# Small-pass evictions shared by ScalarE and VectorE, two additions and one lower sum moved to GpSimd

## The chip, the cores and the metric

The kernel runs on one core of a Trainium2 chip. A core has a matmul engine (PE in the profile, with PEld for the loading of its weights), VectorE (DVE), ScalarE (ACT), GpSimd (POOL), which also issues most of the DMAs here, and SP, which issues the rest. Each engine runs its own list of instructions in the order in which the program wrote them, and semaphores tie the lists together. PE writes only to PSUM, eight banks of 512 float32 values in each of 128 partitions; DVE and ACT read them from there. The metric is the device time in microseconds (us). Before the change it is 955.75 us, the median of three runs (955.62 to 957.78).

## The reference

The input x is 8 batches of 4224 rows of 192 values, float32. First comes a causal convolution along the rows with 7 taps, one set of taps for each of 8 heads of 24 columns; then layer normalisation without a bias, a 192 to 768 to 192 multilayer perceptron with ReLU, and a residual addition.

```python
w = softmax(weight)                              # (8 heads, 7 taps)
y[s, h] = sum(w[h, k] * x[s - 6 + k, h] for k in range(7))
xn = (y - mean(y)) / sqrt(var(y) + 1e-06) * g_ln
out = y + maximum(xn @ w_ch1, 0.0) @ w_ch2
```

## The kernel before, in words

The rows are split over the 128 partitions and worked on in 18 groups; a normal group g has 16 rows in each partition. The kernel works in float32. It folds the mean and g_ln into the first weight matrix, and applies 1/sqrt(var) only at the end, since ReLU lets a positive factor pass.

Groups 3 to 17 are "mixed" (`MIXED`): both matrix products are done by a Strassen-like scheme, with 7 products of quarter matrices in place of 8, and sums of quarters before and after. A mixed group has two stages on PE.

**Up** (`up_mixed`, L611, matmuls on L533) multiplies by the first weights in two passes. The small pass (`one`) makes one block of 128 hidden columns for each quarter: seven products of 24 matmul instructions. The large pass (`two`) makes the other two blocks: seven products of 48. The products go in turn to two sets of four PSUM banks, X and Y, so that PE writes one set while the other is evicted. Some products add to what the other set keeps. After each product ScalarE copies the four banks to the hidden tile `a` (`evict`, L640, its copies on L651). Where two results must be added, the copy goes to a scratch place and POOL issues an accumulating DMA (`close` and `add_by_dma`, L653 and L608), or DVE adds from PSUM (L657).

**Down** (`down_fast`, L833, matmuls on L850) multiplies the hidden tile by the second weights, again with seven products. Before the second, `lower_sum` (L821) has put relu(c21) - c11 in place of c21, in three blocks of 1024 elements a partition. During the fourth product DVE makes three half sums (L817), which the fifth product needs, and then six more. ScalarE copies the results to `cs` (L856), and the fifth and sixth products to `parts`, in places of the hidden tile that are free by then.

The engines do other work at the same time, and its place is written out by hand:

- DVE: taps 2 to 6 of the convolution of group g+1 (`conv`, L417, through `taps_of_next`) in the large pass of g; the transpose of g+1 (L428) in down, ahead of the half sums; at the end of down the sums of quarters s1 and s2 of the next group (`sums_of_y`, L600 and L601) and the batch statistics of its 16 rows (`moments`, L448); then, in the small pass of the next group, `finish_fast` (L908): for either half one addition of `parts` to `cs` (L912) and three transposes to the result tile `ot` (L914).
- ScalarE: the first two taps of group g+2, behind the evictions of down; the ReLUs; the scaling of the finished group by 1/sqrt(var).
- POOL: s3 and s4 (L605, L606), made to wait for DVE's s2 by a tiny memset (L604); the accumulating DMAs: y<-tb (second tap, L409), those of `close`, and those that add the result to the output (L940); in every second group the reciprocal square root for two groups (`root`, `pending`), a chain of some 20 small operations.

`finish_fast` reaches the next group through a generator: `ahead(g)` does both halves when the small pass has been written (L700: `next(ahead)`), so on DVE they come behind the statistics and before the taps of the large pass. The last group (`last`) already shares its small pass, two banks each, between ScalarE and DVE.

Of the kernel before, what the change touches and what calls it, by code (L numbers as in the profile page):

```python
# [11 lines left out]
ALU = mybir.AluOpType  # L12
# [4 lines left out]
def kernel(  # L17
# [29 lines left out]
    nc = tc.nc  # L47
    PSUM = bass.MemoryType.PSUM
    B, S, D = x.shape
    H, K = weight.shape  # L50
# [12 lines left out]
    NQ = P // C  # L63
# [19 lines left out]
    PAIR = NF // 2 - 1  # L83
    HJ = J // 2
    EARLY = 10
    CH = NC // 2
    FC = NF // 2
# [37 lines left out]
    def take_set():  # L125
        i = (turn[0] + 3) // 4 * 4 % 8
        turn[0] = i + 4
        return all_banks[:, i : i + 4]
# [99 lines left out]
    low = consts.tile([P, 1], F32, name="low")  # L228
# [364 lines left out]
    def sums_of_y(g, engine):  # L593

        room = upool.tile([P, 3 * HJ * CH * C], F32, tag="ys", name=f"ysums{g}")
        room = room.rearrange("p (v j c t) -> p v j c t", v=3, c=CH, t=width(g))
        s1, s2, s3 = [room[:, v] for v in range(3)]
        a11, a12, a21, a22 = quarters_of_y(g)
        ysums[g] = s1, s2, s3, a21
        nc.vector.tensor_tensor(s1, a21, a22, op=ALU.add)  # L600
        nc.vector.tensor_tensor(s2, s1, a11, op=ALU.subtract)  # L601
        if engine is not nc.vector:

            nc.vector.memset(s3[:, 0:1, 0:1, 0:1], 0.0)  # L604
        engine.tensor_tensor(s3, a21, a11, op=ALU.subtract)  # L605
        engine.tensor_tensor(a21, a12, s2, op=ALU.subtract)  # L606
# [4 lines left out]
    def up_mixed(g, ahead, pending):  # L611
# [11 lines left out]
        class Pass:  # L623
# [15 lines left out]

            def evict(self, banks, dst, relu=False, f=None):  # L640
                src = self.seen(banks, f)
                if last and self.n == 1:
                    near, far = [[v[:, :, q : q + 2] for v in (dst, src)] for q in (0, 2)]
                    if relu:
                        nc.scalar.activation(*near, AF.Relu)
                        nc.vector.tensor_scalar_max(*far, 0.0)
                    else:
                        nc.scalar.copy(*near)
                        nc.vector.tensor_copy(*far)
                    return  # L650
                nc.scalar.activation(dst, src, AF.Relu) if relu else nc.scalar.copy(dst, src)  # L651
# [23 lines left out]
        def taps_of_next(*args, **kw):  # L675
            if not last:
                conv(g + 1, *args, **kw)


        X, Y = take_set(), take_set()  # L680
        one, two = Pass(PAIR, FC, X, Y), Pass(0, PAIR, Y, X)
        p = one
        p.product(X, a11, p.b11, True, False)
        p.evict(X, p.c11)
        p.product(Y, a12, p.b21)
        p.close(p.c11, Y, two.c12[:, 0:1])
        next(pending, None)
        p.product(X, s2, p.t[0], False, False)
        p.evict(X, p.c21)
        p.product(Y, s3, p.t[1], True, False)  # L690
        p.evict(Y, p.c22)
        p.product(X, s1, p.b12, False, False)
        p.close(p.c22, X, two.c12[:, 1:2])
        next(pending, None)
        p.product(Y, a22, p.t[2], False)
        p.close(p.c21, Y, two.c22[:, 0:1])
        p.product(X, s4, p.b22, False)
        p.evict(X, p.c12, True)

        next(ahead)  # L700
        p = two
        rooms = parts(cpool, "cs"), parts(bpool, "tb")
        p.product(Y, a11, p.b11, True, False)
# [37 lines left out]
        if last:  # L741
            one.relu(one.c22)
        else:
            lower_sum(g, (PAIR,))
            taps_of_next(5, 6, heads=(H // 2, H - 1))
        p.close(p.c21, X)
        if last:
            lower_sum(g, (PAIR,))
# [5 lines left out]
        if last:  # L754
# [9 lines left out]
                nc.scalar.activation(kept[:, f, :, :, h], src, AF.Relu)  # L764

            keeping = [lambda f=f, h=h: keep(f, h) for f in range(NF) for h in range(2)]
        taps_of_next(5, 6, heads=(H - 1, H))
        taps_of_next(6, K)

        def scale_one(j):  # L770
# [47 lines left out]
                a[:, *dst, f], a[:, *left, f], a[:, *right, f], op=op  # L818
            )

    def lower_sum(g, fs=range(FC)):  # L821

        a = of_products(g)
        if g in MIXED:
            for f in fs:
                nc.vector.scalar_tensor_tensor(
                    out=a[:, 1, 0, f], in0=a[:, 1, 0, f], scalar=0.0, in1=a[:, 0, 0, f],
                    op0=ALU.max, op1=ALU.subtract,
                )
        else:  # L830
            half_sum(g, (1, 0), (1, 0), (0, 0), ALU.subtract, fs)

    def down_fast(g, work):  # L833
        n = fast[g]
        t = width(g)
        w = n * T
        a = of_products(g)
        flat = cpool.tile([P, NC, NFAST * C], F32, tag="cs", name=f"cs{g}")[:, :, 0 : n * C]
        order = "p c (h j t) -> p c h j t" if t == C else "p c (j h t) -> p c h j t"
        cs = flat.rearrange(order, h=2, t=t)  # L840
        free = a[:, 1, 0].rearrange("p f q j t -> p (f q) j t")
        parts = [free[:, 0:CH], free[:, CH : 2 * CH]]
        banks = [take_bank() for c in range(CH) for i in range(2)]

        def product(bank, left, right, to, first, behind=0):
            for c in range(CH):
                dst = banks[2 * c + bank]
                for f in (PAIR, *range(PAIR)):
                    for q in range(NQ):
                        nc.tensor.matmul(  # L850
                            dst[C * q : C * q + C, 0:w], right[:, f, C * c : C * c + C],
                            left[:, f, q], start=(first and f == PAIR), stop=(f == PAIR - 1),
                            skip_group_check=True,
                        )
                if to is not None:
                    nc.scalar.copy(  # L856
                        to[:, c], dst[:, 0:w].rearrange("p (j t) -> p j t", t=t)
                    )
                for one in work[:behind]:
                    one()  # L860
                del work[:behind]

        b = quarters_of_w2()
        c11, c21 = cs[:, 0:CH, 0], cs[:, 0:CH, 1]
        c12, c22 = cs[:, CH:NC, 0], cs[:, CH:NC, 1]
        if g == 2:
            work += [lambda h=h: first_tap(4, heads=(h, h + 1)) for h in range(7, H)]
            work += [lambda h=h: second_tap(4, heads=(h, h + 1)) for h in range(H)]
        elif g + 2 < NG:
            work += [  # L870
                lambda tap=tap, h=h: tap(g + 2, heads=(h, h + 1))
                for tap in (first_tap, second_tap) for h in range(H)
            ]
        behind = (1, 1, 1, 1) if g == 2 else (3, 2, 2, 3)
        if g + 1 == NG:
            behind = (0, 0, 1, 2)
        product(0, a[:, 0, 0], b[0], c11, True, behind[0])
        product(1, a[:, 1, 0], w2sums[:, 2], c22, True, behind[1])
        product(1, a[:, 1, 1], w2sums[:, 3], c21, False, behind[2])
        product(1, a[:, 0, 1], b[2], None, True, behind[3])  # L880
        if g + 1 < NG:
            transpose(g + 1)
            if g == 2:
                b11, b12 = quarters_of_w1()[0:2]
                nc.vector.tensor_tensor(b12, b12, b11, op=ALU.subtract)
        half_sum(g, (1, 1), (1, 1), (1, 0), ALU.add)
        half_sum(g, (0, 0), (1, 1), (0, 0), ALU.add)
        half_sum(g, (0, 1), (0, 1), (1, 1), ALU.subtract)
        for c in range(CH):
            nc.vector.tensor_tensor(  # L890
                c11[:, c], c11[:, c], banks[2 * c + 1][:, 0:w].rearrange("p (j t) -> p j t", t=t),
                op=ALU.add,
            )
        product(0, a[:, 1, 1], w2sums[:, 1], parts[0], False, 2)
        product(0, a[:, 0, 0], w2sums[:, 0], parts[1], False, 2)
        for one in work:
            one()
        product(0, a[:, 0, 1], b[3], c12, False)
        if g + 1 < NG:
            sums_of_y(g + 1, nc.gpsimd)  # L900
            if g == 2:
                load_x(5, gate=True)
            moments(g + 1)
        else:
            finish_fast(g, 0, flat, cs, parts)
        return flat, cs, parts

    def finish_fast(g, half, flat, cs, parts):  # L908
        n = fast[g]
        ot = ots[g] if half else out_tile(g)  # L910
        fresh = cs[:, CH * half : CH * half + CH, 1]
        nc.vector.tensor_tensor(fresh, fresh, parts[half], op=ALU.add)  # L912
        for c in range(CH * half, CH * half + CH):
            nc.vector.transpose(  # L914
                ot[:, 0:n, C * c : C * c + C], flat[:, c].rearrange("p (j t) -> p j t", t=C)
            )

    ots = {}

# [76 lines left out]
    def ahead(g):  # L996


        if results is not None:
            for half in range(2):  # L1000
                finish_fast(g - 1, half, *results)
        yield

    w11, w12, w21, w22 = quarters_of_w1()
    b11, b12, b21, b22 = quarters_of_w2()
# [100 lines left out]
```

## Time and profile before

| what | value |
|---|---|
| median of three runs | 955.75 us |
| the profiled execution | 956.96 us |
| its span, first to last instruction | 954.6 us |
| PE, DVE, ACT, POOL busy | 946.8, 894.2, 694.8, 341.8 us |
| up and down stage of a usual mixed group | 27.96 and 27.44 us |
| ACT, eviction of 128x1024 from PSUM (L651), each | 1.013 us |
| DVE, addition of parts (L912), each | 0.929 us |
| DVE, lower sum of one block (L826), each | 1.221 us |
| POOL, 128x768 sum (L605, L606), each | 1.83, 1.82 us |

A line of the trace in order of time gives the start from the beginning of the span, the duration, the engine, the line of the kernel, the operation, what it writes and reads with its shape, and how many such instructions are merged; in brackets stands how long the engine had been idle before, and what ended that wait. Durations of successive DVE instructions overlap by some 0.1 us, so the distance from start to start is the better price of one. A busy PE need not be at its peak, since matmuls are pipelined. A wait is read as: engine and line that waited, what it waited for, us in total, times, longest.

### The profile page before, as it was taken

The page shows a single profiled execution, that of the slowest core. Times are in us where ns is not written, and L with a number is a line of the kernel's source. Part 1 is how long each engine was busy: PE and PEld are TensorE (multiplying, and loading weights), DVE is VectorE, ACT ScalarE, POOL GpSimd, SP SyncE. Part 2 cuts the span into 40 slices and gives each one's busy share as a digit, 9 for nine tenths or more (in the row PEclk, how much of TensorE's full clock was granted, in tenths as well). Part 3 has the DMA queues.
Part 4 walks back from the last instruction along what each step waited for, and adds up shares of the span by engine and source line. Part 5 has one row for each costly group of instructions (what it writes and reads, how often), then busy time and mean ns, then how long its engine had stood idle before and what let it go on. Part 6 is the DMA issues. An engine that isn't in the chain of part 4 may idle for free.

```text
span 954.6 us, 37896 instructions
## 1 busy us (share of the span) xinstructions
PE 946.8 (99%) x16858; PEld 734.5 (77%) x16858; DVE 894.2 (94%) x1496; ACT 694.8 (73%) x1166; POOL 341.8 (36%) x474
## 2 busy tenths in 40 slices
PE   8999999999999999999999999999999999999998
PEld 7998896877869687786958778695867769586787
DVE  8999999999999999999999999999999999999867
ACT  7764678596877959687796968779695877967362
POOL 1158422613145141533227141452316232261330
PEclk9999999999999999999999999999999999999999
DMA  8359589689696988979697897969889697778261
GB/s 206 111 151 218 110 233 269 122 188 226 130 273 131 251 158 185 221 130 278 126 252 152 199 215 128 277 133 249 158 198 206 124 275 134 174 135 141 40 122 68
DMA packets 39832, 169.34 MB, mean 177 GB/s; under 512 B 4469, under 2 KB 8182, under 8 KB 33655
## 3 DMA queue, kind: packets, MB, share of 16 engines
q0 software_dynamic: 32864, 106.77, 60.2%
q1 hardware_dynamic: 6800, 60.16, 17.4%
q8 instruction: 132, 2.16, 0.9%
q14 instruction: 30, 0.25, 0.1%
q10 hardware_dynamic: 6, 0.00, 0.0%
HBM read 38.93 MB, written 50.33 MB: 94 GB/s over the span
## 4 chain that ended last, share of the span: by engine, by line
PE 96%; DMA 1%; POOL 1%; ACT 1%; issue 0%; DVE 0%; ACTq 0%; POOLq 0%
PE ps L533 46%; PE ps L850 44%; PE ps L787 4%; PE ps L367 1%; DMA room<-room 1%; DMA out_dram<-y 1%; PE ps L326 1%; ACT room L651 0%; POOL room L609 0%; POOL d L460 0%; ACT y L380 0%; POOL r L483 0%; POOL d L478 0%; POOL d L479 0%; PE ps L335 0%
## 5 line engine op out<-in xcount | busy, mean ns | idle before, releaser
L417 DVE SCALAR_TENSOR_TENSOR y<-xg,taps,y 128x384 f32<-128x384 f32 (+3 forms) x720 | 364.8, 583 | 2.6 <-DMA y<-room 1.4
L850 PE MATMUL ps<-room,w2sums 128*32 128x256 f32 (+2 forms) x4608 | 246.6, 371 | 0.0
L533 PE MATMUL ps<-yt,w 32*128 32x256 f32 (+2 forms) x4104 | 234.7, 378 | 1.0 <-ACT room L523 0.5
L533 PEld LDWEIGHTS ps<-yt,w 32*128 32x128 f32 x4104 | 204.2, 185 | 26.3 <-issue 8.7
L651 ACT COPY room<-ps 128x1024 f32<-128x1024 f32 (+1 forms) x129 | 169.0, 1310 | 74.5 <-PE ps L533 73.5
L850 PEld LDWEIGHTS ps<-room,w2sums 128*32 128x32 f32 x4608 | 149.3, 110 | 91.5 <-ACT room L664 5.3
L850 PE MATMUL ps<-room,w 128*32 128x256 f32 (+2 forms) x3456 | 188.9, 371 | 0.0
L817 DVE TENSOR_TENSOR room<-room 128x1024 f32<-128x1024 f32 (+2 forms) x147 | 161.2, 1170 | 22.6 <-PE ps L850 16.0
L850 PEld LDWEIGHTS ps<-room,w 128*32 128x32 f32 x3456 | 110.7, 110 | 70.3 <-DVE room L657 5.0
L533 PE MATMUL ps<-ysums,w1sums 32*128 32x256 f32 x2160 | 124.9, 379 | 0.2 <-issue 0.2
L533 PEld LDWEIGHTS ps<-ysums,w1sums 32*128 32x128 f32 x2160 | 109.5, 185 | 10.5 <-ACT room L651 3.3
L940 POOL DMA_DIRECT2D out_dram<-ot x69 | 59.0, 942 | 155.6 <-ACT ot L929 102.5
L409 POOL DMA_DIRECT2D y<-tb x59 | 52.5, 1386 | 153.5 <-ACT room L856 110.1
L856 ACT COPY cs<-ps 128x256 f32<-128x256 f32 (+2 forms) x192 | 70.1, 367 | 45.2 <-PE ps L850 45.2
L664 ACT ACTIVATE room<-room 128x1024 f32<-128x1024 f32 (+1 forms) x89 | 92.5, 1072 | 1.7 <-DMA room<-parts_cs 0.9
L929 ACT ACTIVATE ot<-ot,r 128x192 f32<-128x192 f32 x224 | 90.9, 464 | 0.0
L380 ACT ACTIVATE y<-xg,taps 128x384 f32<-128x384 f32 (+3 forms) x141 | 73.0, 607 | 1.0 <-DMA out_dram<-y 0.7
L448 DVE BATCH_NORM_STATS2 st<-y 128x6 f32<-128x192 f32 x264 | 70.1, 344 | 0.0
L856 ACT COPY room<-ps 128x256 f32<-128x256 f32 (+2 forms) x96 | 35.5, 370 | 45.8 <-PE ps L850 43.8
L398 ACT ACTIVATE tb<-xg,taps 128x384 f32<-128x384 f32 (+1 forms) x120 | 66.1, 628 | 0.0
L533 PE MATMUL ps<-yt,w1sums 32*128 32x256 f32 x1080 | 65.2, 380 | 0.6 <-ACT room L651 0.6
L533 PE MATMUL ps<-ysums,w 32*128 32x256 f32 x1080 | 64.5, 376 | 0.0
(119 smaller groups left out, 924.8 us busy)
## 6 DMA issues: line engine op xcount, KB each, us to landing
xg<-in_x_dram SPq DMA_DIRECT2D x14, 2112.0 KB, 16.4
room<-room POOLq DMA_DIRECT2D x45, 512.0 KB, 5.1
out_dram<-ot POOLq DMA_DIRECT2D x59, 384.0 KB, 9.6
y<-tb POOLq DMA_DIRECT2D x58, 384.0 KB, 8.4
out_dram<-y SPq DMA_DIRECT2D x13, 1536.0 KB, 8.8
room<-parts_cs POOLq DMA_DIRECT2D x28, 512.0 KB, 6.7
room<-parts_tb POOLq DMA_DIRECT2D x14, 1024.0 KB, 7.6
xg<-in_x_dram POOLq DMA_DIRECT2D x1, 2112.0 KB, 13.8
```

The costliest lines, as they stand in the source:

```text
L380: nc.scalar.mul(y[g][:, 0:n, cs], xg[g][:, 0:n, cs], taps[:, h, 0:1])
L398: nc.scalar.mul(tb[g][:, 0:n, cs], xg[g][:, 1 : 1 + n, cs], taps[:, h, 1:2])
L417: nc.vector.scalar_tensor_tensor(out=y[g][:, 0:n, cs], in0=t[:, k : k + n, cs], scalar=taps[:, h, k : k + 1], in1=y[g][:, 0:n, cs], op0=AL ...
L448: nc.vector.bn_stats(out=sums[g][:, j, :], in_=y[g][:, j, :])
L533: nc.tensor.matmul(banks[:, q, i * w : i * w + w], right[rows, c, P * i : P * i + P], left[rows, :, c, :], start=(first and c == 0 and i = ...
L651: nc.scalar.activation(dst, src, AF.Relu) if relu else nc.scalar.copy(dst, src)
L664: nc.scalar.activation(c, c, AF.Relu)
L817: nc.vector.tensor_tensor(a[:, *dst, f], a[:, *left, f], a[:, *right, f], op=op)
L850: nc.tensor.matmul(dst[C * q : C * q + C, 0:w], right[:, f, C * c : C * c + C], left[:, f, q], start=(first and f == PAIR), stop=(f == PAI ...
L856: nc.scalar.copy(to[:, c], dst[:, 0:w].rearrange("p (j t) -> p j t", t=t))
L929: nc.scalar.mul(ots[g][:, j, :], ots[g][:, j, :], rstd[g][:, j : j + 1])
L940: nc.gpsimd.dma_start(out=rows[:, d0:d1], in_=src[:, d0:d1], accum_op=ALU.add)
```

## The change

In every mixed group but the last, the six copies of the small pass are split over the four banks: ScalarE copies three (128x768) and DVE one (128x256). The seventh eviction, with the ReLU, stays with ScalarE, and so do the evictions of the large pass. In the last group nothing changes there.

The two additions of `parts` to `cs` leave DVE for POOL. They are written in `down_fast`, behind the last product: the first ahead of `sums_of_y` (so ahead of s3 and s4 on POOL), the second behind it. The six transposes stay on DVE, but one at a time, one behind each of the six shared evictions (`some_of_last`). In the last group all six follow the small pass as before, and the last group's own result is finished on DVE as before.

The lower sum of the small pass's block leaves DVE for POOL in all mixed groups but the last, as two instructions: a one-input maximum with zero, then a subtraction. On POOL it stands behind the issue of the accumulating DMA that closes c22 of the large pass. Three taps (tap 5 of heads 4 to 6) that DVE did before it adds the last closing product (L657) come behind it.

```diff
--- before.py
+++ after.py
@@ -639,8 +639,11 @@
 
             def evict(self, banks, dst, relu=False, f=None):
                 src = self.seen(banks, f)
-                if last and self.n == 1:
-                    near, far = [[v[:, :, q : q + 2] for v in (dst, src)] for q in (0, 2)]
+                if self.n == 1 and (last or not relu):
+                    cut = NQ // 2 if last else NQ - 1
+                    near, far = [
+                        [v[:, :, qs] for v in (dst, src)] for qs in (slice(0, cut), slice(cut, NQ))
+                    ]
                     if relu:
                         nc.scalar.activation(*near, AF.Relu)
                         nc.vector.tensor_scalar_max(*far, 0.0)
@@ -677,27 +680,38 @@
                 conv(g + 1, *args, **kw)
 
 
+        def some_of_last():
+            if not last:
+                next(ahead, None)
+
         X, Y = take_set(), take_set()
         one, two = Pass(PAIR, FC, X, Y), Pass(0, PAIR, Y, X)
         p = one
         p.product(X, a11, p.b11, True, False)
         p.evict(X, p.c11)
+        some_of_last()
         p.product(Y, a12, p.b21)
         p.close(p.c11, Y, two.c12[:, 0:1])
+        some_of_last()
         next(pending, None)
         p.product(X, s2, p.t[0], False, False)
         p.evict(X, p.c21)
+        some_of_last()
         p.product(Y, s3, p.t[1], True, False)
         p.evict(Y, p.c22)
+        some_of_last()
         p.product(X, s1, p.b12, False, False)
         p.close(p.c22, X, two.c12[:, 1:2])
+        some_of_last()
         next(pending, None)
         p.product(Y, a22, p.t[2], False)
         p.close(p.c21, Y, two.c22[:, 0:1])
+        some_of_last()
         p.product(X, s4, p.b22, False)
         p.evict(X, p.c12, True)
 
-        next(ahead)
+        for _ in ahead:
+            pass
         p = two
         rooms = parts(cpool, "cs"), parts(bpool, "tb")
         p.product(Y, a11, p.b11, True, False)
@@ -741,8 +755,7 @@
         if last:
             one.relu(one.c22)
         else:
-            lower_sum(g, (PAIR,))
-            taps_of_next(5, 6, heads=(H // 2, H - 1))
+            lower_sum(g, (PAIR,), nc.gpsimd)
         p.close(p.c21, X)
         if last:
             lower_sum(g, (PAIR,))
@@ -764,7 +777,7 @@
                 nc.scalar.activation(kept[:, f, :, :, h], src, AF.Relu)
 
             keeping = [lambda f=f, h=h: keep(f, h) for f in range(NF) for h in range(2)]
-        taps_of_next(5, 6, heads=(H - 1, H))
+        taps_of_next(5, 6, heads=(H // 2, H))
         taps_of_next(6, K)
 
         def scale_one(j):
@@ -818,11 +831,18 @@
                 a[:, *dst, f], a[:, *left, f], a[:, *right, f], op=op
             )
 
-    def lower_sum(g, fs=range(FC)):
+    def lower_sum(g, fs=range(FC), engine=nc.vector):
 
         a = of_products(g)
         if g in MIXED:
             for f in fs:
+                if engine is nc.gpsimd:
+                    low = a[:, 1, 0, f]
+                    engine.tensor_scalar(
+                        out=low, in0=low, scalar1=0.0, scalar2=0.0, op0=ALU.max, op1=ALU.add
+                    )
+                    engine.tensor_tensor(low, low, a[:, 0, 0, f], op=ALU.subtract)
+                    continue
                 nc.vector.scalar_tensor_tensor(
                     out=a[:, 1, 0, f], in0=a[:, 1, 0, f], scalar=0.0, in1=a[:, 0, 0, f],
                     op0=ALU.max, op1=ALU.subtract,
@@ -897,7 +917,9 @@
             one()
         product(0, a[:, 0, 1], b[3], c12, False)
         if g + 1 < NG:
+            add_parts(0, cs, parts, nc.gpsimd)
             sums_of_y(g + 1, nc.gpsimd)
+            add_parts(1, cs, parts, nc.gpsimd)
             if g == 2:
                 load_x(5, gate=True)
             moments(g + 1)
@@ -905,15 +927,23 @@
             finish_fast(g, 0, flat, cs, parts)
         return flat, cs, parts
 
-    def finish_fast(g, half, flat, cs, parts):
+    def add_parts(half, cs, parts, engine):
+        fresh = cs[:, CH * half : CH * half + CH, 1]
+        engine.tensor_tensor(fresh, fresh, parts[half], op=ALU.add)
+
+    def transposes_of_last(g, half, flat, cs, parts):
         n = fast[g]
         ot = ots[g] if half else out_tile(g)
-        fresh = cs[:, CH * half : CH * half + CH, 1]
-        nc.vector.tensor_tensor(fresh, fresh, parts[half], op=ALU.add)
         for c in range(CH * half, CH * half + CH):
             nc.vector.transpose(
                 ot[:, 0:n, C * c : C * c + C], flat[:, c].rearrange("p (j t) -> p j t", t=C)
             )
+            yield
+
+    def finish_fast(g, half, flat, cs, parts):
+        add_parts(half, cs, parts, nc.vector)
+        for _ in transposes_of_last(g, half, flat, cs, parts):
+            pass
 
     ots = {}
 
@@ -998,8 +1028,7 @@
 
         if results is not None:
             for half in range(2):
-                finish_fast(g - 1, half, *results)
-        yield
+                yield from transposes_of_last(g - 1, half, *results)
 
     w11, w12, w21, w22 = quarters_of_w1()
     b11, b12, b21, b22 = quarters_of_w2()
```

## The prediction

> **What bounds the kernel now.** I read the page first: who is busy, then the waits of the matmul engine, then one group of 16 rows per partition in order of time.
>
> ```profile
> PE 946.8 (99%) x16858; PEld 734.5 (77%) x16858; DVE 894.2 (94%) x1496; ACT 694.8 (73%) x1166; POOL 341.8 (36%) x474
> ```
>
> PE is busy without a break, and DVE has 6% of idle time. So little can be gained, and DVE can lose little before PE has to wait. In the chain of waits, mixed groups repeat with an up stage of 27.96 us and a down stage of 27.44 us, together 55.40 us:
>
> ```profile
> 311.85 27.62 PE ps L850 x504
> 339.47 27.96 PE ps L533 x504
> 367.43 27.44 PE ps L850 x504
> ```
>
> In the trace by instruction, four matmuls start every 0.216 us in the large pass; 126 such fours would make 27.2 us a stage. The up stage thus wastes 0.76 us, nearly all in its small pass (339.40 to 349.01: 9.61 us where 42 fours need 9.07). What ends it is in the waits of the weight loader:
>
> ```profile
> PEld ps L533 <- ACT room L651: 10.9, 43, 1.0
> ```
>
> That is three short waits a group for ScalarE's eviction, each seen as a late first matmul of a product.
>
> DVE in the same group and the next (start, duration, what; idle before in brackets):
>
> ```profile
> 364.97 2.29 DVE L657 TENSOR_TENSOR room<-room,ps 128x2048 f32<-128x2048 f32 x1 [1.05 <-PE ps L533]
> 367.36 2.36 DVE L826 SCALAR_TENSOR_TENSOR room<-room 128x1024 f32<-128x1024 f32 x2
> 369.64 4.85 DVE L417 SCALAR_TENSOR_TENSOR y<-xg,taps,y 128x384 f32<-128x384 f32 x9
> 374.62 3.38 DVE L428 STREAM_TRANSPOSE yt<-y 128x3072 f32<-128x3072 f32 x1
> 379.02 10.31 DVE L817 TENSOR_TENSOR room<-room 128x1024 f32<-128x1024 f32 x9 [1.02 <-PE ps L850]
> ...
> 390.24 0.95 DVE L600 TENSOR_TENSOR ysums<-yt 128x768 f32<-128x768 f32 x1
> 391.22 0.96 DVE L601 TENSOR_TENSOR ysums<-ysums,yt 128x768 f32<-128x768 f32 x1
> ```
>
> DVE has two points of slack: 1.05 us before it closes c21 (L657) and 1.02 us before the nine half sums (L817). The first three half sums end at 382.51; the fifth product of down needs them and starts at 383.03. From L657 to there the slack is about 1.5 us, and whatever is put between costs PE the excess.
>
> **What the Trainium skill says.** "SBUF — State Buffer", section "SBUF: two separate sides": a pair of SBUF ports is shared by GpSimd and VectorE as an exclusive lock held for the whole instruction; a VectorE operation with two SBUF inputs and a GpSimd operation that reads SBUF block each other. The kernel's own trace agrees, where GpSimd makes differences of weights while DVE does taps:
>
> ```profile
> 72.21 6.37 DVE L417 SCALAR_TENSOR_TENSOR y<-xg,taps,y 128x384 f32<-128x384 f32 x7
> ...
> 71.27 3.16 POOL L582 TENSOR_TENSOR w2sums<-w 128x288 f32<-128x288 f32 x2
> 74.51 2.07 POOL L582 TENSOR_TENSOR w2sums<-w,w2sums 128x288 f32<-128x288 f32 x2
> ```
>
> Seven taps take 6.37 us; the usual start-to-start of one is 0.529 us, so seven need 3.8. DVE lost 2.6 us to four POOL instructions, 0.64 us each. Today's 128x768 POOL sums (L605, L606, 1.83 us each) lie over the batch statistics, which have one input: those keep their 0.260 us.
>
> **The change part by part**, u being the first up matmul, d the first down matmul of a group.
>
> *Evictions split.* Six ScalarE copies of 128x1024 at 1.013 us become 128x768; the line between 128x512 (0.586) and 128x1024 (1.013) gives 0.80, a gain of 0.21 us each, enough to remove the waits: at most 0.6 us a group. DVE gains six copies of 128x256 from PSUM: 128x512 takes 0.692, less 256 elements at 1.04 ns: 0.42 us, 2.5 us in all. A transpose (0.63) follows each, and a product lasts 1.3 us, so from the second on DVE keeps step with PE. Before the first it must finish the statistics, which end at u+1.38, against u+1.64 when the eviction is due: just in time, if nothing delays DVE.
>
> *Additions of the result.* DVE loses 2 x 0.93 us. POOL gains two 128x768 sums of 1.83 us, the first ahead of s3, the second behind s4. Both s3 (fourth product, u+4.1) and s4 (seventh, u+8.2) would still be early.
>
> *Lower sum of the small pass.* DVE loses 1.22 us before L657, where it waits anyway: worth nothing. POOL gains a one-input 128x1024 operation and a two-input one. Of the first the trace has no row: between 0.9 us (POOL's memset of 1152 takes 1.05) and the 2.4 of the two-input one; "GPSIMD Engine Reference", section 4.1, calls one-input work roughly line-rate; I take 1.2. The second follows from 768 elements in 1.83 and 1152 in 2.66: 2.38 us. It waits on POOL behind the issue of the add from parts_tb, which ends at d-2.02. So the pair ends near d+1.65. Down needs it at d+3.9, which holds. But DVE's own two lower sums (two SBUF inputs) are due at d-0.09 and find the lock taken: DVE loses 1.74 us (0.5 to 2.6 over the bounds).
>
> *Taps moved.* Three taps go from before L657, where their 1.59 us was covered by the wait, to behind it, on the path to the half sums. The removed lower sum and these three leave a longer wait at L657, offset by the later small pass of DVE (evictions paced by PE, taps begin at about u+9.5 instead of u+6.9).
>
> Sum at the half sums: 1.59 + 1.74 - 1.02 slack = 2.31 us later than today relative to d. The first three end at d+17.45; with 0.17 to restart, the fifth product begins at d+17.6 instead of d+15.67: **1.95 us of PE stall**.
>
> *A second collision.* The first POOL addition has nothing to wait for but ScalarE's evictions, so it starts when the four issues of y<-tb end, today u-2.87, after L600 and well into L601. With DVE late this changes. Those issues follow ScalarE's taps behind the eviction of the fifth product, 6.02 us after it, and that eviction comes 1.54 us after the product starts, which is 3.66 us after the half sums begin: 11.22 us after them. L600 starts exactly 11.22 us after them today (390.24 - 379.02), L601 12.21. So the POOL sum takes the lock ahead of L600 or L601, and DVE loses 1.83 us. The statistics then end 17.35 + 1.83 = 19.2 us after the half sums, where u is at 15.4; DVE's share of the first eviction ends at u+4.2, and the third product, which writes those banks, wants them by u+2.6: **about 1.7 us of PE stall** (0.1 without the collision).
>
> Sum of a group: 1.95 + 1.7 - 0.6 = +3.05 us. Fourteen groups: 42.7. Before the first mixed group the same POOL addition falls among half sums and the statistics end at u+3.42 even today; its first eviction costs some 2.5 us once. In all +45 us on the span of 954.6, so 1000. The profiled execution took 956.96, its surroundings 2.4 us; the median of before is 1.2 below the profiled time, so I put 45 on 955.75: **1001 us**.
>
> **Rivals.**
> - *Only the first collision.* Should the POOL addition come behind L601 (DVE less late than 0.7 us, or ScalarE behind), the second stall falls to 0.1: 14 x (1.95 + 0.1 - 0.6) + 1 = 21, so 977; with the shortest one-input operation 14 x 1.0 = 970. For it: the two times differ by tenths. Against: either of two DVE sums is enough to collide.
> - *Faster.* The lock does not bite for these shapes, or POOL's instructions slip between. Then the half sums are 1.59 - 1.02 = 0.57 late, against 0.45 of reserve at the fifth product, 0.2 us of stall; gain 0.6: -0.4 to -0.6 a group, 14 groups, 947 to 950. It decides as soon as DVE loses under about 0.4 us to POOL in a group. Against it stand the seven taps above.
> - *POOL's queue is late.* In every second group POOL also carries the root chain; today its third accumulating DMA is issued at u+14.69, and once (727.2) landed late enough to cost PE 0.9 us. The two additions put 1.9 to 3.7 us ahead of it, but the chain would now run over transposes and copies, 0.3 instead of 0.5 us per link; it comes out about as late. If not, 7 x 1 us: 7 more on any case.
> - *The split does not help.* The first matmul after a semaphore could be late whoever evicts: the 0.6 is then 0, 8 us more.
>
> **How the numbers follow.** Both collisions 0.52 (990 to 1010); the first alone 0.24 (966 to 983); faster 0.15 (945 to 952); within 0.3%, which is about what a measurement of this kernel can tell from no change, 0.04; worse than 1010, with POOL's queue late, 0.05. Leaving out the faster and equal ones and the tail leaves 962 to 1010. Slower has 0.81.
>
> **What would show it.** In the changed profile: DVE lower sums (L826's successor) behind L657 with a first one of about 3 us; DVE sums of L600 or L601 of 2.8 us; matmul waits <- DVE at down's fifth product and at the small pass's third; down stages near 29.4 us and up stages near 29. The opposite: ScalarE copies of 0.80 us, an up stage near 27.3 us and down near 27.5. I would be wrong if DVE's two-input operations keep 1.14 us (1024) and 0.95 us (768) while POOL's sums run, or if the one-input POOL operation is so short that the pair ends before d.

## The result, and the profile after

The changed kernel takes 1009.9 us (median of 4 runs, 1007.62 to 1011.47) beside 956.22 us for the kernel before on the same chips: a ratio of 1.056 (95% interval 1.053 to 1.058), 53.7 us slower. The profiled execution took 1010.83 us, its span 1009.1. The head of the page:

```profile
PE 958.3 (95%) x16858; PEld 752.4 (75%) x16858; DVE 945.1 (94%) x1536; ACT 679.5 (67%) x1166; POOL 482.5 (48%) x532
```

DVE is 51 us busier in the record than before, although the change took more work from it than it gave: the surplus is time in which its instructions stood still. The record of the same taps is longer by 29 us, that of the same half sums by 18, that of L600 by 13. PE now has 5% of idle time. Its waits, longest first, were nothing of note before:

```profile
PE ps L870 <- DVE room L830: 31.0, 19, 2.7
PE ps L870 <- POOL room L844: 7.6, 14, 0.6
PE ps L533 <- DVE room L652: 5.8, 8, 0.8
```

L830 are the half sums (L817 before), L844 is GpSimd's subtraction of the lower sum, L652 DVE's bank of an eviction. In the chain of waits PE has fallen from 96% to 58% of the span:

```profile
PE 58%; DVE 22%; POOL 11%; issue 5%; ACT 3%; DMA 1%; DVEq 0%; POOLq 0%; ACTq 0%
```

Here is DVE in order of time around one down stage (d is 385.77), with GpSimd beside it:

```profile
385.77 2.36 DVE L846 SCALAR_TENSOR_TENSOR room<-room 128x1024 f32<-128x1024 f32 x2
388.05 8.56 DVE L417 SCALAR_TENSOR_TENSOR y<-xg,taps,y 128x384 f32<-128x384 f32 x12
396.72 3.38 DVE L428 STREAM_TRANSPOSE yt<-y 128x3072 f32<-128x3072 f32 x1
400.02 10.27 DVE L830 TENSOR_TENSOR room<-room 128x1024 f32<-128x1024 f32 x9
410.21 1.08 DVE L910 TENSOR_TENSOR cs<-cs,ps 128x256 f32<-128x256 f32 x3
411.20 2.58 DVE L600 TENSOR_TENSOR ysums<-yt 128x768 f32<-128x768 f32 x1
...
383.44 3.96 POOL L841 TENSOR_SCALAR room<-room 128x1024 f32<-128x1024 f32 x1
387.49 2.89 POOL L844 TENSOR_TENSOR room<-room 128x1024 f32<-128x1024 f32 x1
...
407.58 3.52 POOL L409 DMA_DIRECT2D y<-tb  x4 [9.09 <-ACT tb L398]
409.76 3.20 POOL L932 TENSOR_TENSOR cs<-cs,room 128x768 f32<-128x768 f32 x1
```

Twelve taps beside L844 take 8.56 us; elsewhere in this trace twelve take 6.43. The first tap has all of the difference: it takes 2.74 us instead of 0.61 and ends 0.42 after L844. L600 beside GpSimd's first addition (L932) takes 2.58 us where it took 0.95. The half sums follow the transpose at once, so the slack of 1.02 us ahead of them is used up. In the next group the same addition, as late after the first half sum to within 0.02 us, gets in ahead of the ninth half sum instead, and the nine take 14.01 us rather than 10.3. The ninth alone takes 4.96 us instead of 1.22; its record begins 0.68 us before the addition's and ends 1.09 after it, so VectorE was shut out before the record of the addition begins:

```profile
458.35 14.01 DVE L830 TENSOR_TENSOR room<-room 128x1024 f32<-128x1024 f32 x9
...
468.08 3.18 POOL L932 TENSOR_TENSOR cs<-cs,room 128x768 f32<-128x768 f32 x1
```

Such a down stage takes 32.4 to 34.1 us (27.44 before), one of the first kind 29.5, in seven groups with an up stage of 28.8 behind it. Five groups of fourteen went the second way.

Where the time went follows from the starts of the products, summed over the fourteen down stages and fifteen up stages and compared with before. Down's second product starts late by 10.2 us in all, its fifth by 20.3 more, its seventh by 14.2 (these five groups) and the end of down by 4.8; the third product of the small pass is longer by 7.1. The other products of the small pass, with the first of the large one behind it, gained 6.2, the rest of the large pass lost 3.9, and with smaller differences this makes 53.5 of the 54.5 us by which the span grew.

### The profile page after: what moved, and what is told of

It reads as the page before. It is cut to its first block, busy times and chain, and to the rows that moved or that the text cites. A ratio compares the mean times of both kernels' runs of the same rounds, so it can differ in the third digit from the quotient of the medians.

```text
span 1009.1 us, 38091 instructions
## 1 busy us (share of the span) xinstructions
PE 958.3 (95%) x16858; PEld 752.4 (75%) x16858; DVE 945.1 (94%) x1536; ACT 679.5 (67%) x1166; POOL 482.5 (48%) x532
## 4 chain that ended last, share of the span: by engine, by line
PE 58%; DVE 22%; POOL 11%; issue 5%; ACT 3%; DMA 1%; DVEq 0%; POOLq 0%; ACTq 0%
PE ps L533 34%; PE ps L870 18%; DVE room L830 14%; POOL room L841 6%; POOL room L844 4%; PE ps L800 4%; DVE st L448 3%; ACT parts_tb L654 3%; DVE ysums L600 2%; PE ps L367 1%; DVE cs L910 1%; DVE ysums L601 1%; DMA room<-room 1%; PE ps L326 1%; DVE room L652 0%
## 5 line engine op out<-in xcount | busy, mean ns | idle before, releaser
L417 DVE SCALAR_TENSOR_TENSOR y<-xg,taps,y 128x384 f32<-128x384 f32 (+3 forms) x720 | 393.4, 621 | 2.4 <-DMA y<-room 1.4
L533 PEld LDWEIGHTS ps<-yt,w 32*128 32x128 f32 x4104 | 212.0, 185 | 20.7 <-issue 6.2
L830 DVE TENSOR_TENSOR room<-room 128x1024 f32<-128x1024 f32 (+2 forms) x147 | 179.3, 1292 | 8.3 <-ACT kept L777 6.6
L533 PE MATMUL ps<-ysums,w1sums 32*128 32x256 f32 x2160 | 134.5, 379 | 5.8 <-DVE room L652 5.8
L533 PEld LDWEIGHTS ps<-ysums,w1sums 32*128 32x128 f32 x2160 | 118.9, 185 | 13.4 <-DVE room L652 10.0
L651 ACT COPY room<-ps 128x768 f32<-128x768 f32 (+1 forms) x90 | 70.6, 784 | 64.9 <-PE ps L533 64.9
L654 ACT COPY room<-ps 128x2048 f32<-128x2048 f32 x45 | 83.9, 1864 | 30.6 <-PE ps L533 30.1
L932 POOL TENSOR_TENSOR cs<-cs,room 128x768 f32<-128x768 f32 (+1 forms) x30 | 74.9, 2497 | 10.7 <-ACT room L876 10.7
L533 PE MATMUL ps<-ysums,w 32*128 32x256 f32 x1080 | 71.5, 374 | 0.0
L533 PE MATMUL ps<-yt,w1sums 32*128 32x256 f32 x1080 | 71.3, 375 | 0.0
```

What stands on the lines that cost most here:

```text
L417: nc.vector.scalar_tensor_tensor(out=y[g][:, 0:n, cs], in0=t[:, k : k + n, cs], scalar=taps[:, h, k : k + 1], in1=y[g][:, 0:n, cs], op0=AL ...
L533: nc.tensor.matmul(banks[:, q, i * w : i * w + w], right[rows, c, P * i : P * i + P], left[rows, :, c, :], start=(first and c == 0 and i = ...
L830: nc.vector.tensor_tensor(a[:, *dst, f], a[:, *left, f], a[:, *right, f], op=op)
L932: engine.tensor_tensor(fresh, fresh, parts[half], op=ALU.add)
```

## The experiments

Theory: GpSimd and VectorE hold the shared port against each other, so the two moves to GpSimd stretch VectorE's two-input sums. Main rival: VectorE and the pacing by evictions are simply too much work, whoever does the sums. A second rival: GpSimd's own queue is late. An edit below is one to the changed kernel where nothing else is said.

**The lower sum undone.**

```diff
-            lower_sum(g, (PAIR,), nc.gpsimd)
+            lower_sum(g, (PAIR,))
```

> The changed kernel with one thing undone: the lower sum of the small pass is one VectorE instruction again; evictions, additions on GpSimd and the moved taps stay. Theory (the shared port is a lock, and GpSimd's two lower-sum instructions cost VectorE about 2.1 us and delay down's second product by 0.7): down's second product no longer waits (first product 3.9 us instead of 4.63), the fifth product's stall falls from 1.4 to about 0.2, the additions still collide with L600 or a half sum (1.0 us a group or more); 14 x about 2 us less, so 978 to 986 us. Rival (VectorE simply has too much work, whoever does the lower sum): VectorE gets 1.2 us a group back, so the time rises by up to 14 x 1.2 to about 1025.

Measured: 991.59 us, ratio 1.036 (1.034 to 1.037); better than the change by 18 us with more work on VectorE. Down's second and fifth products are back to their old lengths, as the theory says and against the first rival. The time is 5.6 us above the range expected, because the other collision grew: the third product of the small pass is longer by 29.5 us over all groups instead of 7.1. VectorE and GpSimd in one of them:

```profile
459.80 3.95 DVE L600 TENSOR_TENSOR ysums<-yt 128x768 f32<-128x768 f32 x1
...
457.53 3.53 POOL L409 DMA_DIRECT2D y<-tb  x4 [8.31 <-ACT room L876]
459.71 3.21 POOL L932 TENSOR_TENSOR cs<-cs,room 128x768 f32<-128x768 f32 x1
```

L932 stands in the record for 3.21 us, though alone it takes 1.82: for the first 1.35 GpSimd is still issuing the DMAs ahead of it (until 461.06). L600 waits through all of it and ends 0.83 after it, about the 0.95 that it takes alone. So the sum shuts VectorE out for 3.1 us, not 1.83. The issues alone don't do this. In the kernel before, the same four lie over L600 at 390.24 and over L601, and both keep their 0.95 and 0.96 us:

```profile
388.38 3.54 POOL L409 DMA_DIRECT2D y<-tb  x4 [8.30 <-ACT room L856]
```

**The additions undone.**

```diff
-            add_parts(0, cs, parts, nc.gpsimd)
             sums_of_y(g + 1, nc.gpsimd)
-            add_parts(1, cs, parts, nc.gpsimd)
...
             for half in range(2):
+                add_parts(half, *results[1:], nc.vector)
                 yield from transposes_of_last(g - 1, half, *results)
```

> The changed kernel with the two additions of the result back on VectorE, each ahead of its three transposes; the lower sum stays on GpSimd. Theory (lock): no addition on GpSimd near the half sums, so no sum of 2.6 or 5 us on VectorE, the small pass's third product back to 1.3 us, no down stage of 34 us; the lower sum's cost stays (first product of down 4.63, fifth product late by 1.4 or more, since VectorE's taps start about 1 us later): 975 to 985 us. Rival (work, not the lock): VectorE has 1.9 us more to do in a group, so about 1010 + 14 x 1.9 = 1036.

Measured: 987.49 us, ratio 1.032 (1.030 to 1.033); the rival's 1036 is out. No half sum and no L600 is stretched, no down stage is over 29.9 us. What remains is the lower sum's part, 10.4 us at down's second and 20.6 at its fifth product. VectorE took back 28 additions of 0.93 us and the kernel became 22 us faster.

**The same work, another order on GpSimd.**

```diff
-            add_parts(0, cs, parts, nc.gpsimd)
             sums_of_y(g + 1, nc.gpsimd)
+            add_parts(0, cs, parts, nc.gpsimd)
             add_parts(1, cs, parts, nc.gpsimd)
```

> The changed kernel with the first addition moved behind s3 and s4 on GpSimd, next to the second; every engine does the same work as in the changed kernel, only GpSimd's order differs. Theory (lock): the additions now lie over VectorE's one-input work, so VectorE's L600, L601 and half sums keep 0.95 and 1.14 us, and 14 x about 2 us go away; the first transpose waits for GpSimd until about 2.9 us into the small pass, which may cost 0.3 us of it back: 978 to 988 us. Rival (work on VectorE or GpSimd): same work, so 1005 to 1013. Rival (the race at the ninth half sum is something else than the addition): stages of 34 us stay.

Measured: 987.6 us, ratio 1.032 (1.030 to 1.034). Every engine has the work of the changed kernel; only when GpSimd adds has changed, and 22 us are gone, with the stages of 34 us. Its groups by shape show both at their own price, GpSimd's additions and VectorE's L600:

```profile
L932 POOL TENSOR_TENSOR cs<-cs,room 128x768 f32<-128x768 f32 x28 | 50.3, 1819 | 0.0
...
L600 DVE TENSOR_TENSOR ysums<-yt 128x768 f32<-128x768 f32 x15 | 14.2, 948 | 0.0
```

In the changed kernel these means were 2550 and 1822 ns. This run decides against any account by amount of work. The later additions have a small price of their own: the first transpose waits for them, and the fourth product of the small pass is longer by 0.2 us a group, 3.0 in all.

**The price of the one-input operation.** To the kernel before, behind s3:

```diff
         engine.tensor_tensor(s3, a21, a11, op=ALU.subtract)
+        if engine is nc.gpsimd:
+            engine.tensor_scalar(
+                out=s3, in0=s3, scalar1=-1e30, scalar2=0.0, op0=ALU.max, op1=ALU.add
+            )
```

> The kernel before with one GpSimd instruction more in each mixed group: a one-input maximum and addition over s3 in place (128x768, it changes nothing in the values), while VectorE does its one-input statistics. It measures the disputed price. If the 3.97 us of 128x1024 are GpSimd's own, this takes about 2.97 us; if they came from waiting for VectorE, 0.8 to 1.3 us. s4 then comes 1 to 3 us later, still ahead of the seventh product, and the time stays within 1 us of 956 (a few us more if the third accumulating DMA of a group with the root chain lands later).

```profile
L607 POOL TENSOR_SCALAR ysums<-ysums x15: 2768/2777/2786, 118.9 to 895.0; 128x768 f32<-128x768 f32 x15
```

The view of this line gives shortest, median and longest in ns: 2.78 us for 768 elements, in all 15 groups. Most of it lies beside VectorE's one-input statistics; the last 0.8 us lie over VectorE's addition of `parts`, which has two SBUF inputs and keeps its 0.94 us. So it is GpSimd's own price, 3.6 ns an element, and above the two-input sum of the same size (1.83). At this price 1024 elements take 3.70 us. Of the 3.96 us of L841 above, 0.29 lie under the DMA issue ahead of it, which ends at 383.73; the 3.67 that are left are thus its own, and none of them is waiting. The kernel with it takes 957.87 us, ratio 1.001 (1.000 to 1.002).

**The split alone**, on the kernel before, with everything else on VectorE in its old order but for the additions and transposes, which stand between the evictions:

```diff
-                if last and self.n == 1:
-                    near, far = [[v[:, :, q : q + 2] for v in (dst, src)] for q in (0, 2)]
+                if self.n == 1 and (last or not relu):
+                    cut = NQ // 2 if last else NQ - 1
...
+        some_of_last()
...
-                finish_fast(g - 1, half, *results)
-        yield
+                add_parts(half, *results[1:], nc.vector)
+                yield from transposes_of_last(g - 1, half, *results)
```

> The split of the evictions alone: additions back on VectorE (ahead of their transposes, which still stand between the evictions), lower sum and the three taps back in their old places on VectorE. Theory: no lock is in play, but VectorE is now paced by the small pass until about 10.5 us and does its taps, lower sum and three taps after it, so it comes to the closing sum (c21) about 3 us late and down's first product waits for it; the small pass gains 0.5: 14 x 2 to 2.5, so 984 to 991 us. Rival (the split itself is free and the moves to GpSimd did all the harm): 946 to 952.

Measured: 974.97 us, ratio 1.020 (1.018 to 1.021). The direction is the theory's: the split isn't free. The size is not, and the time is 9 us below the range expected: the taps began 9.55 us into the up stage, not 10.5, and down, which waits for the closing sum, began 1.85 us late and not some 3. The waits of the weight loader show the place:

```profile
PEld ps L871 <- DVE room L660: 27.2, 15, 2.0
```

The small pass, with the product behind it, gained 7 us in all, and the last product of up, which ends where down begins, became 25 us longer in all.

**Both collisions taken away**: late additions, and the lower sum on VectorE (the first and third edits together).

> The changed kernel with both of its collisions taken away: the first addition behind s3 and s4 on GpSimd, and the lower sum of the small pass on VectorE. Theory (lock): no VectorE sum is longer than usual, no stall at down's second product; what remains are the three taps moved behind the closing sum (up to 0.2 us at the fifth product), 0.3 us for the first transpose and the closing sum 0 to 0.5 late, against 0.6 won in the small pass: 952 to 960 us. Rival (the two parts hurt by VectorE's work, not by the lock): above 970.

Measured: 959.23 us, ratio 1.002 (1.001 to 1.003). Of the 53.7 us 51 are gone with the two collisions. The 18 us of the split alone are not found here: the additions are on GpSimd and three taps stand behind the closing sum, so it is late no more, and up stages take 28.1 us instead of 29.4.

**ReLU on ScalarE**: on top of the late additions, the maximum leaves GpSimd.

```diff
+        if not last:
+            one.relu(one.c21)
         for f in range(PAIR):
             p.relu(p.c11[:, f : f + 1])
...
-                    engine.tensor_scalar(
-                        out=low, in0=low, scalar1=0.0, scalar2=0.0, op0=ALU.max, op1=ALU.add
-                    )
```

> As the run with the late additions, but the maximum of the lower sum is a ReLU on ScalarE, ahead of the two ReLUs of c11, so GpSimd has only the subtraction. Theory: GpSimd starts it at about d-1.8 (d: down's first matmul) and ends at d+0.6 to d+1.0, so down's second product no longer waits (3.9 instead of 4.63), and VectorE, blocked until then only, loses 0.5 to 1.0 us instead of 2.1: the fifth product's stall falls from 1.4 to 0.4 to 0.9. 14 x 1.3 to 1.8 less than 987.6, so 962 to 970. Rival (the 3.97 us of the one-input instruction are harmless, being beside single-input work): 985 to 988.

Measured: 962.06 us, ratio 1.006 (1.005 to 1.008). The subtraction now runs at d-2.2 to d+0.4, over the closing sum, which has one SBUF input:

```profile
422.74 2.51 POOL L843 TENSOR_TENSOR room<-room 128x1024 f32<-128x1024 f32 x1
...
422.49 2.29 DVE L660 TENSOR_TENSOR room<-room,ps 128x2048 f32<-128x2048 f32 x1 [1.07 <-PE ps L533]
424.88 2.60 DVE L845 SCALAR_TENSOR_TENSOR room<-room 128x1024 f32<-128x1024 f32 x2
```

The closing sum keeps its 2.29 us; the two lower sums lose 0.24. Down's second product no longer waits, and the fifth is late by 0.2 us a group instead of 1.45.

**A version fitted to this.** On top of the run before: no transpose behind the first eviction and two behind the third, and two of the three moved taps ahead of the closing sum again.

```diff
         p.evict(X, p.c11)
-        some_of_last()
...
         p.evict(X, p.c21)
         some_of_last()
+        some_of_last()
...
-        taps_of_next(5, 6, heads=(0, H // 2))
+        taps_of_next(5, 6, heads=(0, H // 2 + 2))
...
-        taps_of_next(5, 6, heads=(H // 2, H))
+        taps_of_next(5, 6, heads=(H // 2 + 2, H))
```

> A version fitted to the lock: additions late, ReLU on ScalarE and subtraction on GpSimd as in the run before, no transpose behind the first eviction and two behind the third, and two of the three moved taps back ahead of the closing sum (30 taps there). Theory: the half sums start no later than PE's third product of down ends plus 0.45, so no stall at the fifth product; up stages near 27.4 and down stages near 27.5 us: 946 to 952 us, faster than both kernels. If the subtraction still overlaps VectorE's two lower sums for more than 0.8 us, or the taps make the closing sum late: 953 to 962.

Measured: 955.52 us, ratio 0.9986 (0.9975 to 0.9996), in the second of the ranges that were expected, but for a cause not named there. Half of the groups have stages of 27.41 and 27.44 us as intended. The up stages of the others, those with the root chain, lost up to 1.9 us each, 5.1 in all, 4.5 of them in one place, ahead of the sixth product of the large pass. The waits say what ScalarE's evictions (L654) stood for:

```profile
ACT room L654 <- DMA room<-room: 5.7, 6, 2.0
```

This is the second rival, the late queue: with the two additions ahead, GpSimd comes to its root chain later and issues the small pass's third accumulating DMA behind it at u+15.6 instead of u+14.7 (u: up's first matmul), and ScalarE may not overwrite that DMA's source before it has landed.

**That DMA ahead of the chain**, on the fitted version and on the kernel before:

```diff
-        next(pending, None)
         p.product(Y, a22, p.t[2], False)
         p.close(p.c21, Y, two.c22[:, 0:1])
+        next(pending, None)
```

> The fitted version with one more move: in the groups with the root chain, GpSimd issues the third accumulating DMA of the small pass (c21) before the second part of the chain, not after it. Theory: in the fitted version the up stages of these groups lose 0.3 to 1.9 us (5.1 in all) because this DMA lands late and ScalarE's eviction of c22 waits for it; issued some 5 us earlier it lands in time, all up stages are 27.4 us: 955.5 - 5 = 949 to 952 us, ratio 0.992 to 0.996. Rival (something else makes these stages long, or the chain now delays the scaling of the result and with it ScalarE): no change, 954 to 957.

> The kernel before with this one reordering only. Theory: before has lost 0.9 us once to that DMA, so 0.5 to 1 us less, no difference that can be told; the gain of the run beside it is not from the reordering alone. Rival (the reordering itself is worth as much in the kernel before): 950 to 953.

Measured: the fitted version 949.4 us, ratio 0.992 (0.991 to 0.993); the kernel before with the reordering alone 956.8, ratio 1.000 (0.999 to 1.001). The chain of waits of the fitted version:

```profile
447.19 27.41 PE ps L533 x504
474.60 27.45 PE ps L869 x504
502.04 27.41 PE ps L533 x504
```

A pair of stages takes 54.86 us instead of 55.40. This version beats both kernels, by 7.7 us the one before and by some 60 the changed one. The late queue thus accounts for 6 us of the run before it, and in the kernel before, where it was late once, the reordering is worth no difference that can be told.

## Why the prediction was right, point by point

The forecast was 1001 us, slower, 962 to 1010; measured were 1009.9, slower by 53.7 where 45 were forecast. The likeliest case, both collisions, is the one that occurred, and it was shown by undoing either and by the order alone. The mechanism was right; that the time fell inside the range, by 0.1 us, was in part luck, since some terms were off in opposite directions. By its steps:

- *What bounds the kernel, and the slack of DVE.* Right: once the half sums begin without a wait, each delay appears in PE.
- *Evictions split.* The small pass gained 0.44 us a group (6.2 in all) of the 0.6 forecast; DVE's share takes 0.42 us as forecast. That the rest of up would lose 3.9 us was not foreseen, and its cause stays open. Together they are the largest miss, 0.16 us a group where 0.6 were counted on. The 0.76 us that up wasted before were also not nearly all in the small pass: 0.54 were, and 0.2 in the first and last product of the large one.
- *Lower sum.* The one-input operation was taken at 1.2 us, at most 2.4; it takes 3.67, three times as long. So "down needs it at d+3.9, which holds" failed: the pair ends at d+4.6, and down's second product waits 0.73 us a group. VectorE's loss was forecast at its lower sums and 1.74 us; it came at the taps and was 2.13. With the wait ahead of it, the fifth product lost 1.45 instead of 1.95. The two together are 2.18 a group, near the 1.95 forecast. By the trace the wait at the second product hides in the other: the third half sum ends at d+17.71, and the fifth product, which needs it, starts at d+17.76 (forecast d+17.6), so it would have started no earlier without that wait. That the sum held in spite of the wrong price is luck. Had the longer operation also held the lock when VectorE's lower sums were due, VectorE would have lost some 4.1 us (an estimate: from d-0.09 to the end of the pair at -2.02 + 3.67 + 2.38 = d+4.03). It did not hold it, and the two errors cancelled.
- *Second collision.* Right in place, mis-sized in the hold: the addition was to take the lock for 1.83 us when the issues end, and shuts VectorE out from before that, for up to 3.7 us. In seven groups the small pass lost 0.9 instead of the 1.7 forecast: VectorE's copy ended at u+3.95 (forecast u+4.2), and PE went on with the other three banks before it waited. In five the ninth half sum was hit, which was not foreseen for these groups, and cost PE 2.9 to 4.6 us. On average 1.87 us a group; that this is near 1.7 is luck again.
- *The first mixed group* was to lose 2.5 us more; its up stage lost 0.5.
- *Rivals.* The chance for the faster case rested on the lock not biting; it does. The late queue cost one stage of the changed kernel 0.4 us, but 5.1 us in the fitted version, where nothing else hid it.

What the Trainium skill says in "SBUF — State Buffer", section "SBUF: two separate sides", was borne out for two-input sums on both sides: the one that comes second stands still for the whole of the other. It was not for the one-input maximum: GpSimd's L841 ran from 383.44 to 387.40, and VectorE's two-input L846 beside it kept 2.36 us for two. The Trainium skill's "GPSIMD Engine Reference", section 4.1, has one-input work at roughly line rate; here it takes 3.6 ns an element against 2.4 for a two-input sum. In both points the measurement decides.

Not settled is what tips the addition ahead of the ninth half sum in five groups and behind it in the others; the starts in the record agree to 0.02 us. Nor is it settled from when a sum that stands behind DMA issues holds the lock.

## What to carry to other kernels

Two-input work that goes from VectorE to GpSimd should lie, in time, over VectorE instructions with at most one SBUF input; in these runs copies from PSUM, transposes, statistics and sums with a PSUM operand kept their length beside it. Beside two-input sums VectorE lost here about what GpSimd spent, and more where the GpSimd instruction stood behind DMA issues. An engine that takes part in an eviction is paced by PE, and what it did back to back before then ends later, as the split alone showed: count the time to its next due point, not its busy time. When one wait goes, look at the DMAs that were issued just in time behind it.

## What the runs showed of the hardware

- GpSimd's one-input tensor_scalar with maximum and addition takes 2.78 us for 768 float32 a partition and 3.67 for 1024 (3.97 in the record, with the end of a DMA issue under it); its two-input sum takes 1.82 for 768 and 2.5 for 1024, or 2.9 where it first waits for a two-input VectorE sum.
- That one-input instruction did not hold up two-input VectorE work: two lower sums kept 2.36 us beside it, an addition 0.94.
- A two-input GpSimd sum behind DMA issues blocked a two-input VectorE sum for 3.1 us, 1.3 of them before the issues had ended, and in another place for 3.7. The issues alone left such sums at 0.95 us.
- GpSimd's subtraction left VectorE's sum of an SBUF and a PSUM operand at 2.29 us.
